# Q, K and V of two blocks by seven block products, in a phase of their own

## The chip, the cores and the metric

The kernel runs on one core of a Trainium2 chip. Its time is the device time of one execution in microseconds (us). Five engines work side by side, each through its own instructions in order: TensorE (PE, matmuls; its weight loads are shown as PEld), VectorE (DVE), ScalarE (ACT), GpSimd (POOL) and SyncE (SP, which here only issues DMAs). They wait for each other by semaphores.

## The reference

One transformer block whose attention and feed-forward parts are both added to the input (S = 2048 tokens, D = 576, 32 heads of 18, F = 4608, float32):

```python
xn = layernorm(x)
q, k, v = split_heads(xn @ wqkv)              # wqkv: 576 x 1728
# each token attends to itself and 7 earlier ones, 2 apart (0, 2, ..., 14 back)
attn = softmax(q . k[pos - 2 w] * 18 ** -0.5)  # masked where pos - 2 w < 0
a = (sum over w of attn * v[pos - 2 w]) @ wo
h = relu(xn @ w1 + b1) ** 2                    # 4608 wide
out = x + a + h @ w2 + b2
```

## The kernel before

**Numbers in two parts.** Matmuls read float32 in a rounded form (F32R). To keep the precision, an operand v is split into hi = rounded v (a ScalarE copy) and lo = v - hi (a DVE subtraction), and a product is hi*hi + lo*hi + hi*lo: three matmuls. So every weight that TensorE reads costs one ScalarE and one DVE operation: `w2_hi`/`w2_lo` for a tile of w2, `h_hi`/`h_lo` for a pair of tiles of the hidden activations that comes back from DRAM, `wq_hi`/`wq_lo` for wqkv.

**Tiles.** The 2048 tokens are four blocks of 512 (b = 0 to 3). D = 576 is four chunks of 128 and a left part of 64 (`x4`), which carries hi and lo in its 128 rows. wqkv is in four groups g of eight heads, 432 columns each (q, k and v of 144). The result is kept transposed, so that out is D x S.

**FFN1** (`ffn_pair`, L524 and L528) takes two blocks at a time and multiplies [two blocks] x [two halves of D] x [two tiles of w1] as a 2 x 2 by 2 x 2 block product in seven products instead of eight. It needs sums of blocks of x (`sums`, `last_sum`: SS[1..3], the fourth in X[b1][:, :, :2]) and of the weights (`combine_w1`; the slots T1, T3, B11, T2, B22, B21, T4), and some additions on the way out. FFN2 (`tile_products`, L493) is plain: 14 matmuls of 512 columns for each of the 36 tiles of F.

**The order.** It is written out by hand. Each engine does its instructions in the order of the code:

1. `open_rows` and `q0`: Q, K, V of blocks 0 and 1 (`qkv_row`, L304).
2. `phase_a(0)`: FFN1 of blocks 0 and 1 in 18 pairs of tiles, with FFN2 of block 0 in between; the activations of block 1 go to DRAM (`hscr`). Then Wo of block 0 and `finish(0)`: five drains on DVE (L747) of the sums in PSUM into the residual, and the stores.
3. `phase_b0`: FFN2 of block 1 over 36 tiles n, from DRAM, and in between the 32 rows of Q, K, V of blocks 2 and 3 (2 blocks x 4 groups x 4 row tiles j; 14 matmuls of 432 columns each, then a ScalarE copy into `st` and a DMA to `kvq`, L296 and L298). Then Wo of block 1; its last products and `finish(1)` are handed to the next phase as a `filler`.
4. `phase_a(1)`: the same as 2 for blocks 2 and 3.
5. `phase_b1`: FFN2 of block 3, Wo, and the end.

**What fills DVE.** Attention reads q, k and v of one block and group from DRAM (`kvq`) and works on DVE alone but for the exponential. `attention(b, g)` is a generator of 18 steps: four of q-k product (L95, `pr<-q,kv`) and four reductions (L353), two of softmax, four weightings (`pr<-lg,kv`) and four sums with the output. `side(k)` takes the next k steps from a queue of such generators; `complete(b)` forces all that is left of a block; then `regroup(b, .)` loads the output back and `o_hi`/`o_lo` turn it for Wo. `run(pieces, k)` takes k steps from a list `pieces` of other generators first: in `phase_b0` these are `normalize(2)`, the load of the statistics `mb` of block 3, `normalize(3)` (8 steps each), the splits of wqkv, and `sums(1)` (12 steps). Every tile n there takes `w2_hi`, `h_hi` (even n), the 14 matmuls, `w2_lo`, `h_lo` (even n), and then the steps of `run`. The buffers `w2s`, `h` and `w1s` are three deep, `w1r` two, `r4` four; PSUM has eight banks (`bank(0..7)`), and FFN2's sums of block 1 hold 5, 6, 7, 0, 1 (`YB`).

In `phase_b0` the rows are let in by the line

```python
while r < 32 and 32 * (n - 6) > 22 * r:
```

so from tile 7 to tile 28, more than one a tile.

Of the kernel before, what the change touches and what calls it, by code (L numbers as in the profile page):

```python
# [8 lines left out]
F32 = mybir.dt.float32  # L9
# [3 lines left out]
ALU = mybir.AluOpType  # L13
# [32 lines left out]
def block_kernel(ctx: ExitStack, tc: tile.TileContext, x, xt, wqkv, wo, w1, b1, w2, b2, out):  # L46
# [47 lines left out]
    def tt(out, a, b, op):  # L94
        return nc.vector.tensor_tensor(out=out, in0=a, in1=b, op=op)  # L95
# [196 lines left out]
    def open_stage():  # L292
        stage[0] = sb.tile([P, NJ, QW], F32, name="st")
# [93 lines left out]
    def side(k, exp=True):  # L387

        while k > 0:
            if current[0] is None:  # L390
                if not queue or queue[0][0] not in landed:
                    return k
                name, make = queue.pop(0)
                current[:] = [make(), None, name]
            if current[1] == "exp" and not exp:
                return k
            try:
                current[1] = next(current[0])
                k -= 1
            except StopIteration:  # L400
                current[0] = None
        return 0
# [17 lines left out]
    def once(f, *a):  # L420
        f(*a)
        return
        yield
# [80 lines left out]
    def ffn_pair(s, p, work, first=False):  # L504
# [179 lines left out]
    ob = {}  # L684

    def regroup(b, k):
        if k == 0:
# [6 lines left out]
    ot, of = {}, {}  # L694

    def o_hi(b, c):
        if c % 2 == 0:
            ot[b, c // 2] = mt.tile([P, 2, 2, TB], F32R, name="w1s", bufs=3)
# [8 lines left out]
        nc.vector.transpose(t[:, 0].rearrange("p (u k f) -> p u k f", k=2, f=n),  # L707
                            ob[b, 1][:, :, None, OB - n:].to_broadcast([P, NJ * G, 2, n]))
        nc.scalar.activation(t[:, 1].bitcast(F32R), t[:, 0], AF.Copy)

    def o_lo(b, c):
        hi, lo = (ot[b, c // 2][:, c % 2, k] for k in range(2))
        t = of.pop((b, c))
        if c < NC - 1:
            tt(lo, t[:, 0], hi.bitcast(F32), ALU.subtract)
# [19 lines left out]
    def open_left(b):  # L735
        xr[b].append(four()[:, 0])
# [7 lines left out]
    def drain(b, c, ts=slice(0, TB)):  # L744
        n = P if c < NC - 1 else D - DM
        o = kept(b, c, ts)
        i = nc.vector.scalar_tensor_tensor(out=o, in0=yp[b][c][:n, ts], scalar=b2t[:n, c:c + 1], in1=o,  # L747
                                           op0=ALU.add, op1=ALU.add)
        if c == NC - 1:
            i = tt(o, yp[b][c][n:2 * n, ts], o, ALU.add)  # L750
        return i

    def finish(b):
        for c in range(NC):
            drain(b, c)
# [13 lines left out]
    def h_lo(s, p):  # L769
        if p < NP:  # L770
            t = hs[s, p]
            tt(t[:, 1], t[:, 1].bitcast(F32), t[:, 0].bitcast(F32), ALU.subtract)

    def phase_b0():
        b, r = 1, 0
        todo = [(2 + i, g, j) for g in range(G) for i in range(2) for j in range(NJ)]
        split_up.clear()
        open_stage()
        load_wq(0)
        pieces = [normalize(2), once(load_mb, 3), split_wq(0, "S", lambda: load_wq(1)), normalize(3)]  # L780
        open_y(b)
        for n in range(NF):
            w2_hi()
            if n % 2 == 0:
                h_hi(0, n // 2 + 1)
            add(b, tile_products(b, n, hs[0, n // 2]))
            w2_lo()
            if n % 2 == 0:
                h_lo(0, n // 2 + 1)
            if n % 2 and n // 2 + 3 < NP:  # L790
                load_h(0, n // 2 + 3)
            run(pieces, 1 + n % 2 if n < 9 else 1)
            while r < 32 and 32 * (n - 6) > 22 * r:
                bb, g, j = todo[r]
                while bb not in normed or g not in split_up:
                    run(pieces, 1)
                qkv_row(bb, g, j, 2 + r % 3)
                r += 1
                if r == 2:
                    pieces.append(split_wq(1, "w1s", lambda: load_wq(2)))  # L800
                if r == 8:
                    pieces.append(split_wq(2, "S", lambda: load_wq(3)))
                if r == 16:
                    pieces.append(split_wq(3, "w1s"))
                if r == 24:
                    pieces.append(sums(1))
                if j == NJ - 1 and bb == 2:
                    offer(2, g)
                run(pieces, 2)
            if n == 3:  # L810
                load_xt(3)
            if n == 20:
                load_w1(NP)
            if n == 25:
                assert not any(a != "x" and c < 2 for a, c, _ in loads)
                held[0] = True
            if n == 28:
                run_all(pieces)
                last_sum(1)
                complete(1)  # L820
                regroup(b, 0)
                regroup(b, 1)
                held[0] = False
                fetch()
                load_w1(NP + 1)
                for g in range(G):
                    offer(3, g)
            if n == 31:
                combine_w1(NP)
            if n == 33:  # L830
                residual(b)
            if n in (32, 33):
                c = 2 * (n - 32)
                o_hi(b, c), o_hi(b, c + 1)
                o_lo(b, c), o_lo(b, c + 1)
        o_hi(b, 4)
        o_lo(b, 4)
        open_left(b)
        load_left(b)
        for c in range(3):  # L840
            w2_hi()
            add(b, o_ops(b, c))
            w2_lo()
            if c == 1:
                w1_hi(NP, 0)
                w1_lo(NP, 0)

        def filler(i):
            if i < 2:
                add(b, o_ops(b, 3 + i), range(NC) if i else ())  # L850
            if i == 0:
                w1_hi(NP, 1)
                w1_lo(NP, 1)
            if i == 1:
                finish(b)

        return filler

# [379 lines left out]
```

## Time and profile before

| | us |
|---|---|
| median of 3 runs | 1127.12 (1125.72 to 1128.43) |
| profiled execution | 1125.13 |
| its span | 1123.4 |
| PE / PEld / DVE / ACT busy | 1112.8 / 938.1 / 914.7 / 575.7 |
| FFN2 of block 1 with the QKV rows | about 436.6 to 640.7 |

In the profile, "L95" is the helper `tt` (any DVE operation of two tensors), "L493" the matmuls of FFN2 and Wo, "L304" those of `qkv_row`. A row of a group has: line, engine, operation, tile written <- tiles read, shapes, count | busy us, mean ns of one | idle time of the engine just before them and what ended it. A row of a wait has: who <- for whom, total us, times, longest. A row of a window has: its start and end, length, then busy time of PE, PEld, DVE, ACT and POOL with instruction counts, the granted clock of TensorE (1.00 is full), the share of the DMA engines and GB/s. A row of the timeline has: start, duration, engine, line, and in brackets the idle time before it and what ended it. A row of the chain has start, duration and what; in the view of a tile one row gives the time of its DMAs from issue to landing.

### The profile page before, as it was taken

The page shows a single profiled execution, that of the slowest core. Times are in us where ns is not written, and L with a number is a line of the kernel's source. Part 1 is how long each engine was busy: PE and PEld are TensorE (multiplying, and loading weights), DVE is VectorE, ACT ScalarE, POOL GpSimd, SP SyncE. Part 2 cuts the span into 40 slices and gives each one's busy share as a digit, 9 for nine tenths or more (in the row PEclk, how much of TensorE's full clock was granted, in tenths as well). Part 3 has the DMA queues.
Part 4 walks back from the last instruction along what each step waited for, and adds up shares of the span by engine and source line. Part 5 has one row for each costly group of instructions (what it writes and reads, how often), then busy time and mean ns, then how long its engine had stood idle before and what let it go on. Part 6 is the DMA issues. An engine that isn't in the chain of part 4 may idle for free.

```text
span 1123.4 us, 13847 instructions
## 1 busy us (share of the span) xinstructions
PE 1112.8 (99%) x5014; PEld 938.1 (84%) x5014; DVE 914.7 (81%) x1202; ACT 575.7 (51%) x801; POOL 117.7 (10%) x219
## 2 busy tenths in 40 slices
PE   8999999999999999999999999999999999999998
PEld 7998888888888888899888888888888888888887
DVE  6696998897978887789888979898988988786463
ACT  5434656656566654542342455666556666533341
POOL 4000201020300210002011001020202011001000
PEclk9999999999999999999999999999999999999999
DMA  8854645384573648766674845354545362568653
GB/s 292 310 188 130 203 162 199 111 212 155 175 198 104 252 180 303 257 231 213 215 247 145 318 154 194 144 172 149 202 140 203 112 217 94 186 200 305 181 169 90
DMA packets 88965, 216.50 MB, mean 193 GB/s; under 512 B 11960, under 2 KB 40384, under 8 KB 83520
## 3 DMA queue, kind: packets, MB, share of 16 engines
q1 hardware_dynamic: 52464, 148.95, 39.0%
q0 software_dynamic: 10544, 52.14, 14.4%
q10 hardware_dynamic: 25888, 14.53, 4.3%
q8 instruction: 39, 0.64, 0.2%
q14 instruction: 30, 0.25, 0.1%
HBM read 173.03 MB, written 42.55 MB: 192 GB/s over the span
## 4 chain that ended last, share of the span: by engine, by line
PE 87%; DVE 6%; DMA 3%; ACT 2%; issue 1%; SPq 0%; ACTq 0%; POOL 0%; DVEq 0%; POOLq 0%
PE p L493 42%; PE p L524 29%; PE p L304 9%; PE p L528 5%; DVE pr L95 1%; PE p L1022 1%; DMA kvq<-st 1%; DVE w1s L95 1%; DMA kv<-kvq 1%; DMA w2r<-in_w 1%; DVE r L95 1%; DVE lg L353 0%; DVE w1r L95 0%; DVE w2s L95 0%; DMA r<-in_wqkv 0%
## 5 line engine op out<-in xcount | busy, mean ns | idle before, releaser
L493 PE MATMUL p<-h,w2s 128*128 128x512 f32 x2010 | 484.4, 390 | 0.7 <-ACT h L535 0.2
L493 PEld LDWEIGHTS p<-h,w2s 128*128 128x128 f32 x2010 | 376.8, 188 | 81.2 <-ACT h L535 1.2
L524 PE MATMUL p<-X,w1s 128*128 128x512 f32 x864 | 219.5, 389 | 2.6 <-DVE w1s L95 2.6
L524 PEld LDWEIGHTS p<-X,w1s 128*128 128x128 f32 x864 | 162.1, 188 | 36.5 <-DVE w1s L95 3.0
L466 ACT ACTIVATE w2s<-w2r 128x640 fp32r<-128x640 f32 x164 | 120.1, 734 | 110.6 <-PE p L493 92.9
L95 DVE TENSOR_TENSOR w2s<-w2r,w2s 128x576 fp32r<-128x576 f32 x164 | 123.4, 754 | 63.8 <-ACT w2s L466 61.7
L524 PE MATMUL p<-S,w1s 128*128 128x512 f32 x648 | 164.6, 389 | 0.0
L524 PEld LDWEIGHTS p<-S,w1s 128*128 128x128 f32 x648 | 121.4, 188 | 25.5 <-DVE r L95 0.2
L381 POOL DMA_DIRECT2D o<-q x128 | 69.3, 606 | 606.5 <-DVE q L95 604.6
L95 DVE TENSOR_TENSOR w1s<-w1r,w1s 128x1024 fp32r<-128x1024 f32 x72 | 88.0, 1223 | 27.7 <-ACT w1s L439 27.6
L531 ACT ACTIVATE r<-r,b1t 128x512 f32<-128x512 f32 x72 | 51.9, 721 | 105.8 <-DVE r L95 105.7
L95 DVE TENSOR_TENSOR pr<-q,kv 128x1152 f32<-128x1152 f32 x64 | 86.8, 1356 | 1.5
L296 ACT ACTIVATE st<-p 128x432 f32<-128x432 f32 x64 | 33.8, 528 | 104.5 <-PE p L304 89.7
L95 DVE TENSOR_TENSOR pr<-lg,kv 128x1152 f32<-128x1152 f32 x64 | 86.6, 1353 | 0.7
L353 DVE TENSOR_REDUCE lg<-pr 128x64 f32<-128x1152 f32 x64 | 86.4, 1349 | 0.9
L95 DVE TENSOR_TENSOR pr<-pr 128x576 f32<-128x576 f32 (+1 forms) x128 | 77.7, 607 | 3.8
L439 ACT ACTIVATE w1s<-w1r 128x1024 fp32r<-128x1024 f32 x72 | 75.7, 1052 | 5.1 <-PE p L493 4.2
L539 ACT ACTIVATE r<-r 128x1024 f32<-128x1024 f32 x72 | 75.5, 1051 | 0.1
L95 DVE TENSOR_TENSOR h<-r,h 128x1024 fp32r<-128x1024 f32 (+2 forms) x42 | 49.2, 1180 | 30.2 <-ACT r L539 23.7
L528 PE MATMUL p<-x,w1s 128*128 128x512 f32 x216 | 66.5, 389 | 0.0
L95 DVE TENSOR_TENSOR r<-p,r 128x512 f32<-128x512 f32 (+1 forms) x76 | 52.2, 687 | 13.2 <-ACT r L589 10.3
L304 PE MATMUL p<-w1s,X 128*128 128x432 f32 x288 | 60.3, 358 | 0.0
(138 smaller groups left out, 1114.0 us busy)
## 6 DMA issues: line engine op xcount, KB each, us to landing
w2r<-in_w SPq DMA_DIRECT2D x144, 320.0 KB, 3.2
kv<-kvq POOLq DMA_DIRECT2D x29, 1296.0 KB, 6.8
w1r<-in_w SPq DMA_DIRECT2D x36, 640.0 KB, 4.4
h<-r SPq DMA_DIRECT2D x36, 512.0 KB, 2.9
h<-h SPq DMA_DIRECT2D x36, 512.0 KB, 4.1
kvq<-st ACTq DMA_DIRECT2D x64, 216.0 KB, 3.1
r<-in_wqkv SPq DMA_DIRECT2D x16, 432.0 KB, 5.5
w2r<-in_wo SPq DMA_DIRECT2D x20, 320.0 KB, 3.0
```

What stands on the lines that cost most here:

```text
L95: return nc.vector.tensor_tensor(out=out, in0=a, in1=b, op=op)
L296: nc.scalar.activation(stage[0][:, j], p[:, :QW], AF.Copy)
L304: nc.tensor.matmul(p[:, :QW], l, r, start=k == 0, stop=k == len(mm) - 1)
L353: nc.vector.tensor_reduce(out=lg[:, j * HG:(j + 1) * HG].rearrange("p a w -> p w a"), in_=pr.rearrange("p w (a d) -> p w a d", d=DH), axis ...
L381: nc.gpsimd.dma_start(rows[:, i], q[i * L:(i + 1) * L, :, a:z])
L439: nc.scalar.activation(w1s[n, k][:, 0], raw1[n][:, 4 * k:4 * k + 4], AF.Copy)
L466: nc.scalar.activation(w2s[stream[i]][:, :DE], raw2[i], AF.Copy)
L493: nc.tensor.matmul(yp[b][c], v, a, start=c not in yb[b], stop=c in last and c not in [o[0] for o in ops[i + 1:]], skip_group_check=True)
L524: nc.tensor.matmul(to, l, r, start=start and i == 0, stop=i == len(mm) - 1, skip_group_check=True)
L528: nc.tensor.matmul(to, weight(LEFT, k, f), v, start=False, stop=k == 1, skip_group_check=True)
L531: nc.scalar.activation(to, a, AF.Relu, bias=b1t[:, f:f + 1])
L539: nc.scalar.activation(r, r, AF.Square)
```

## The change

The 32 rows leave the loop of FFN2 of block 1. Behind that loop comes a phase of its own for Q, K, V of blocks 2 and 3: [block 2, block 3] x [two halves of D] x [groups 2k, 2k + 1] by the same seven products that FFN1 uses, for k = 0, 1 and each of the four row tiles j. `quad_step(k, s, j, i)` does step s for one j; two j run side by side (i = 0, 1), in banks 2, 3, 4, 0 and 5, 6, 7, 1. So a "half" is two row tiles of one k, and there are four halves. The sums of x are those that FFN1 needs anyhow; the weights are combined and split into eight slots on DVE and ScalarE (`first_slots`, `third_slot`, `split_slot`, `split_side`), for k = 0 within the FFN2 loop, for k = 1 during the phase.

As the phase takes all eight banks, the sums of FFN2 of block 1 are drained first into the residual, go to DRAM (`yscr`, `yleft`), and come back before Wo of block 1, which then adds without the bias (`finish(b, False)`). Attention of block 1 gives up to one more step a pair in FFN1 of blocks 0 and 1 (`side(3)`), and its `complete(1)` comes in the second half of the phase; block 2 is offered from there on, block 3 behind the phase. The splits of w1 for the next FFN1 move into the phase. `regroup(1)` uses one `kv` buffer, and `o_hi` of block 1 `h` buffers.

The diff, cut to its core:

```diff
         if not first:
-            side(1 if p == 1 else 2 + p % 2, False)
+            side(1 if p == 1 else 2 + p % 2 if s else 3, False)
...
+    def first_slots(k):
+        v, b12 = raw[k, 0][:, 0], raw[k, 0][:, 1]
+        b21, b22 = raw[k, 1][:, 0], raw[k, 1][:, 1]
+        if not k:
+            split_slot(B11, v)
+            yield
+        tt(v, b12, v, ALU.subtract)
+        yield
+        split_slot(T1, v)
+        yield
+        tt(v, b22, v, ALU.subtract)
+        yield
+        split_slot(T2, v)
+        yield
+        tt(v, b21, v, ALU.subtract)
+        yield
+
+    def third_slot(k):
+        v = raw[k, 0][:, 1]
+        tt(v, raw[k, 1][:, 1], v, ALU.subtract)
+        split_slot(T3, v)
...
+    def quad_step(k, s, j, i):
...
+        def product(to, name, v, start=False):
+            mm = [(v(0, n), ws[name][0][:, n]) for n in range(2)]
+            for n in range(2):
+                mm += [(v(0, n), ws[name][1][:, n]), (v(1, n), ws[name][0][:, n])]
...
+        def row(n, f, x, y=None):
+            st = stage[0][:, rows_out[0] % NJ]
+            rows_out[0] += 1
+            nc.scalar.activation(st, x, AF.Copy)
+            if y is not None:
+                tt(st, y, st, ALU.add)
...
+        if s == 1:
+            product(a, B11, lambda h, q: X[b0][:, h, q], start=True)
+            nc.scalar.activation(b, a, AF.Copy)
+        if s == 2:
+            product(c, T1, ss(1), start=True)
+        if s == 3:
+            product(b, T2, ss(2))
+            nc.scalar.activation(u, b, AF.Copy)
+        if s == 4:
+            left(c, 1, x4[b1])
+            product(b, T3, ss(3))
+            row(b1, 1, b, c)
+        if s == 5:
+            product(a, B21, lambda h, q: X[b0][:, h, 2 + q])
+            left(a, 0, x4[b0])
+            row(b0, 0, a)
+        if s == 6:
+            product(c, B22, lambda h, q: X[b1][:, h, q])
+            left(c, 1, x4["d"])
+            row(b0, 1, c, u)
+        if s == 7:
+            product(b, T4, lambda h, q: X[b1][:, h, 2 + q])
+            left(b, 0, x4[b1])
+            row(b1, 0, b)
...
     def phase_b0():
...
-        pieces = [normalize(2), once(load_mb, 3), split_wq(0, "S", lambda: load_wq(1)), normalize(3)]
+        pieces = [normalize(2), once(load_half, 0, 0), once(load_mb, 3), normalize(3), once(load_sides, 0), sums(1),
+                  once(load_half, 0, 1), once(last_sum, 1), first_slots(0), once(third_slot, 0),
+                  once(split_side, 0, 0), once(split_side, 0, 1)]
...
-            run(pieces, 1 + n % 2 if n < 9 else 1)
-            while r < 32 and 32 * (n - 6) > 22 * r:
...
+            run(pieces, 1 + n % 2)
...
             if n == 33:
                 residual(b)
+                xr[b].append(sb.tile([P, TB], F32, name="xf"))
+                load_left(b)
+            if n == 34:
+                split_slot(B21, raw[0, 1][:, 0])
+        for c in range(NC):
+            drain(b, c)
+            if c in (1, 3):
+                nc.sync.dma_start(yscr[:, c - 1:c + 1], xr[b][0][:, c - 1:c + 1])
+        nc.sync.dma_start(yleft, kept(b, NC - 1))
+        open_stage()
...
+        for k in range(2):
+            for half in range(2):
+                for s, i in ((1, 0), (1, 1), (2, 0), (2, 1), (3, 0), (3, 1), (5, 0), (4, 0), (5, 1), (4, 1),
+                             (7, 0), (6, 0), (7, 1), (6, 1)):
+                    quad_step(k, s, 2 * half + i, i)
+                    hook(k, half, s, i)
+                    if (s, i) in ((2, 0), (2, 1), (3, 0), (5, 0), (5, 1), (4, 1), (7, 0), (7, 1)) and (k, half) != (0, 1):
+                        side(1, s == 7)
...
+        xr[b] = [mt.tile([P, NC - 1, TB], F32, name="h", bufs=3)]
+        nc.sync.dma_start(xr[b][0], yscr)
+        open_y(b)
         for c in range(3):
             w2_hi()
             add(b, o_ops(b, c))
             w2_lo()
...
             if i == 1:
-                finish(b)
+                finish(b, False)
```

`hook` puts the loads and splits of the weights of k = 1, T4 and B22 of k = 0, `complete(1)`, the offers of block 2, and the first work for Wo of block 1 and for the next FFN1 behind single steps of the phase: in the first half T4 behind step 1 and B22 behind step 5 (i = 0), in the second half the slots of k = 1.

More of the change, by code (lines that the diff above doesn't have):

```diff
@@ L686, in regroup @@
     def regroup(b, k):
+        if b == 1:
+            assert free[0]
+            free[0] -= 1
+            t = sb.tile([P, NJ * G * CG], F32, name="kv", bufs=3)
+            for i, n in enumerate((OA, OB)):
+                ob[b, i] = t[:, i * NJ * G * OA:][:, :NJ * G * n].rearrange("p (r c) -> p r c", c=n)
+                nc.gpsimd.dma_start(t[:, i * NJ * G * OA:][:, :NJ * G * n], oscr[b, i].rearrange("p r c -> p (r c)"))
+            return
         if k == 0:
@@ L772, in h_lo, with load_half, load_sides @@
             tt(t[:, 1], t[:, 1].bitcast(F32), t[:, 0].bitcast(F32), ALU.subtract)
+    raw, ws, yscr = {}, {}, dram.tile([P, NC - 1, TB], F32, name="y1")
+    yleft = dram.tile([D - DM, TB], F32, name="y1e")
+    def load_half(k, i):
+        t = raw[k, i] = sb.tile([P, 2, 2, QW], F32, name="w1r", bufs=2)
+        for f in range(2):
+            nc.sync.dma_start(t[:, f], wqkv[2 * k + f, :, 2 * i:2 * i + 2])
+    def load_sides(k):
+        t = raw[k, "left"] = sb.tile([P, 2, QW], F32, name="mb")
+        for f in range(2):
+            nc.sync.dma_start(t[:, f], wqkv[2 * k + f, :, NC - 1])
@@ new lines, in slot, with split_slot, split_side @@
+    def slot(name):
+        if name == B11:
+            ws[name] = [four(F32R)[:, :, :QW] for _ in range(2)]
+        else:
+            t = mt.tile([P, 2, 2, TB], F32R, name="w1s" if name in (T1, T2, T3) else "h", bufs=3)
+            ws[name] = [t[:, i, :, :QW] for i in range(2)]
+        return ws[name]
+    def split_slot(name, v):
+        split(*slot(name), v)
+    def split_side(k, f):
+        t = ws[LEFT, f] = four(F32R)[:, :, :QW]
+        split(t[:, 0], t[:, 1], raw[k, "left"][:, f])
@@ new lines, in phase_b0 @@
+        for k in range(2):
[6 more added lines that the diff above has]
+                        side(1, s == 7)
+                    if (s, i) in ((2, 1), (5, 0), (7, 0)) and (k, half) == (0, 1):
+                        side(1, s == 7)
@@ L840, in phase_b0 @@
+        for g in (2, 3):
+            offer(2, g)
+        for g in range(G):
+            offer(3, g)
+        xr[b] = [mt.tile([P, NC - 1, TB], F32, name="h", bufs=3)]
+        nc.sync.dma_start(xr[b][0], yscr)
+        open_y(b)
         for c in range(3):
```

147 lines of the change are left out of this document (87 added, 60 removed).

## The prediction

> **What bounds the kernel now.** I read the page first, then the chain of waits in order of time, the waits of each engine, and the groups of instructions by form for VectorE (DVE).
>
> ```profile
> PE 1112.8 (99%) x5014; PEld 938.1 (84%) x5014; DVE 914.7 (81%) x1202; ACT 575.7 (51%) x801; POOL 117.7 (10%) x219
> PE p L524 <- DVE w1s L95: 2.6, 1, 2.6
> ...
> 615.69 2.75 PE p L304 x14
> 618.44 22.25 PE p L493 x98
> ```
>
> TensorE is busy for 99% of the span, and its longest wait for data in the middle of the kernel is 2.6 us. So time comes off only with matmuls. One QKV row (14 matmuls of 432 columns, L304) takes 2.75 us, 196 ns each; a tile of FFN2 (14 matmuls of 512, L493) takes 22.25 / 7 = 3.18 us. The other half of the reading is DVE in the stage that changes:
>
> ```profile
> 440.00:640.60 200.60, 200.45 (x941) 176.39 (x939) 174.90 (x202) 78.83 (x114) 19.55 (x36) 1.00 0.69 236
> ```
>
> In FFN2 of block 1 with QKV of blocks 2 and 3 strewn in, TensorE (second number) never waits, but DVE (fourth) is busy for 174.9 of 200.6 us: 87%, with 26 us to spare. TensorE is slow enough for DVE only because of the QKV rows.
>
> **The matmuls removed.** Before: 2 blocks x 4 groups x 4 row tiles x 14 = 448 matmuls. After: 8 calls of the seven products x (7 x 6 + 8 for the left part) = 400. Forty-eight fewer at 196 ns: **-9.4 us**, all of it on TensorE's path.
>
> **What DVE has to do before the new phase can start.** The banks 5, 6, 7, 0, 1 of FFN2's sums are needed by the new phase; its second product (step 1 with i = 1) writes bank 5, which only DVE's first drain frees. DVE works in order, so that drain stands behind everything queued in the 36 tiles. TensorE's own road to that product is 36 x 3.18 + 6 x 0.196 = 115.7 us from the first FFN2 matmul (436.6 us). DVE's road I add up. Its start is the same list as before, up to the end of `normalize(2)`, and the trace shows it:
>
> ```profile
> 436.55 2.72 DVE L747 SCALAR_TENSOR_TENSOR w1r<-p,b2t,w1r 128x512 f32<-128x512 f32 x4
> ...
> 449.24 1.22 DVE L95 TENSOR_TENSOR w1r<-w1r,mb 128x1024 f32<-128x1024 f32 x1
> 452.21 0.76 DVE L95 TENSOR_TENSOR w2s<-w2r,w2s 128x576 fp32r<-128x576 f32 x1 [1.75 <-ACT w2s L466]
> ...
> 459.63 0.69 DVE L95 TENSOR_TENSOR x<-xf,x 64x512 fp32r<-64x512 f32 x1
> 460.35 1.06 DVE L95 TENSOR_TENSOR S<-r,S 128x864 fp32r<-128x864 f32 x1
> DVE w2s L95 <- ACT w2s L466: 2.6, 3, 1.8
> DVE h L95 <- ACT h L767: 0.4, 2, 0.2
> ```
>
> That is 23.8 us for six tiles' worth: block 0's drains, six `w2_lo`, three `h_lo`, one `normalize`, and 3.0 us of waits for ScalarE. Their durations add to 21.7, so 0.9 overlaps (4%). What follows, by form:
>
> ```profile
> L95 DVE TENSOR_TENSOR w2s<-w2r,w2s 128x576 fp32r<-128x576 f32 x164 | 123.4, 754 | 63.8 <-ACT w2s L466 61.7 <-PE p L304 1.3 <-issue 0.2
> L95 DVE TENSOR_TENSOR h<-h 128x1024 fp32r<-128x1024 f32 x36 | 44.0, 1223 | 5.4 <-ACT h L767 5.1 <-DMA kvq<-st 0.2
> L95 DVE TENSOR_TENSOR w1r<-w1r,mb 128x1024 f32<-128x1024 f32 x12 | 14.4, 1220 | 2.3 <-DMA mb<-mr 2.1
> L95 DVE TENSOR_TENSOR r<-r,mb 128x512 f32<-128x512 f32 x2 | 1.4, 688 | 0.0
> L95 DVE TENSOR_TENSOR S<-r,S 128x864 fp32r<-128x864 f32 x6 | 6.2, 1055 | 5.1 <-ACT S L262 5.1
> L95 DVE TENSOR_TENSOR S<-r,S 128x432 fp32r<-128x432 f32 x3 | 1.8, 604 | 0.5 <-ACT S L262 0.5
> L95 DVE TENSOR_TENSOR pr<-q,kv 128x1152 f32<-128x1152 f32 x64 | 86.8, 1356 | 1.5
> L353 DVE TENSOR_REDUCE lg<-pr 128x64 f32<-128x1152 f32 x64 | 86.4, 1349 | 0.9
> L95 DVE TENSOR_TENSOR pr<-lg,kv 128x1152 f32<-128x1152 f32 x64 | 86.6, 1353 | 0.7
> L95 DVE TENSOR_TENSOR pr<-pr 128x576 f32<-128x576 f32 (+1 forms) x128 | 77.7, 607 | 3.8
> L95 DVE TENSOR_TENSOR q<-pr 128x144 f32<-128x144 f32 x64 | 19.7, 308 | 2.2
> L363 DVE TENSOR_REDUCE sm<-lg 128x32 f32<-128x256 f32 x16 | 6.7, 418 | 6.6 <-ACT lg L361 6.6
> L95 DVE TENSOR_TENSOR lg<-lg,mx 128x256 f32<-128x256 f32 x16 | 6.8, 425 | 0.5
> 414.29 1.36 DVE L95 TENSOR_TENSOR pr<-q,kv 128x1152 f32<-128x1152 f32 x1
> ```
>
> - 30 `w2_lo` x 0.754 = 22.6; 14 `h_lo` x 1.223 = 17.1.
> - `normalize(3)`: six operations of 1024 at 1.22 and three of 512 at 0.69 = 9.4.
> - `sums(1)`, `last_sum`: eleven of 1024 and two of 512 = 14.8.
> - The weight slots B11, T1, T2, T3, B21: five differences `lo` and four weight differences of 864 at 1.055, and two sides of 432 at 0.604 = 10.7.
> - Attention. The loop takes 1 + n % 2 steps a tile, 54 in all; the list uses 34 (8 + 8 + 12 + 6) and leaves 20. Before, when FFN1 of blocks 0 and 1 ends, attention of block 1 stands at the first step of its third group (the q-k product at 414.29), and counting the yields of the generators gives the same place; with `side(3)` in the even pairs the place is 7 steps further on. The 20 steps are then two softmaxes, four q-k with reductions, four weightings with sums: 4 x (1.356 + 1.349 + 1.353 + 2 x 0.607 + 0.308) + 2 x 2.04 (five operations of about 0.41) = 26.4.
>
> Together 101.0, less 4% overlap 97.0. To this come two waits that the list makes:
>
> *The statistics of block 3.* `normalize(3)` follows `normalize(2)` at once, and its first operation needs `mb`, whose load stands on SP behind two new loads of 432 KB.
>
> ```profile
> 460.05 0.38 SPq L762 DMA_DIRECT2D h<-h  x1
> 460.48 0.42 SPq L172 DMA_DIRECT2D mb<-mr  x1
> DVE w1r L95 <- DMA mb<-mr: 1.8, 1, 1.8
> DMA to landing us min/median/max: 6.7/6.8/8.7
> 436.00:463.00 27.00, 23.93 (x28) 1.00 0.81 280
> ```
>
> Before, DVE filled that time with the first weight split and still waited 1.8 us. After, SP reaches `mb` two issues later, about 461.3; 6.7 us more is 468.0, a wait of 7.7 us from 460.3; 864 KB ahead of it at the window's 280 GB/s make 3.1 more, 10.8. I take 10. The Trainium skill ("DMA: Bandwidth & Descriptors", Anatomy of one DMA) puts a transfer at about 2.0 us plus its bytes over 436 GB/s. By it the three would need an estimated 5.2 us, the wait would be about 6 and the sum 4 us less; the trace's 6.7 for `mb` alone, against 3.2 by that fit, disagrees.
>
> *ScalarE in between.* ScalarE is in order too. Where a tile's last step ends with a copy on ScalarE, the next `w2_hi` stands behind the copy, and DVE waits for both: the 1.75 us at 452.21. This happens when DVE is what lags. `normalize(3)` meets it three times (5 us), `sums` three times (5); the splits of T2 and T3 follow their own difference at once (1 each), the two softmaxes cost 0.55 each (6.6 us for 12 waits), `h_hi` about 1: 14, between 5 (most of it met by time already lost) and 18.
>
> DVE's road: 23.8 + 97.0 + 10 + 14 = 144.8, and the first drain 0.7: 145.5 against TensorE's 115.7. TensorE cannot keep ahead, since `w2s` and `h` are three deep: the hi part for tile n + 2 is freed by tile n - 1, so it can lead DVE by about two tiles, 6.4 us. Behind the last `w2_lo` that TensorE needs, DVE has about 9 us of steps before the first drain, and TensorE only 3.2 us of work (2 of FFN2, 1.2 of the first product): some 5.5 us of the loss show as a wait at the new phase's start, the rest as waits inside FFN2. **+29.8 us**; with the ends of the two waits, 12.8 + 5 below and 10.8 + 18 above, +18 to +35.
>
> **The new phase itself.** Each half has 100 matmuls, 19.6 us. DVE there: half 1 the five drains (4.2), T4 and B22 (2.1), eight steps (11.5), four additions (about 2.5) = 20.3; half 2 the slots of k = 1, 15.5; halves 3 and 4 some 14 each. Its additions free a bank only 24 matmuls (4.7 us) later, so a lag of that size is hidden: nothing in the middle, up to 3 us if half 1 runs late. Sums to DRAM: two stores of 512 KB, under way 5.8 us after the drains begin, before the slot that they hold is wanted by B22 (about 7.5). The load back has the 13 us of Wo. At the end, bank 7 and bank 1 wait for a ScalarE copy (528 ns) and an addition: **+0.6**. Attention of blocks 2 and 3 moves behind: FFN1 is as full as before (DVE 88%), and FFN2 of block 3 gets steps for 20 tiles instead of 10. There two tiles cost DVE about 6.8 us against 6.36: **+0.5**, between 0 and 2, hidden by the same lead. `side(3)` in FFN1 of block 0: nothing, DVE has 14% spare there.
>
> ```profile
> L296 ACT ACTIVATE st<-p 128x432 f32<-128x432 f32 x64 | 33.8, 528 | 104.5 <-PE p L304 89.7 <-DMA kvq<-st 10.8 <-ACT st L296 2.4
> 200.00:300.00 100.00, 100.00 (x443) 82.81 (x442) 86.08 (x139) 60.67 (x81) 16.21 (x27) 1.00 0.52 154
> 880.00:940.00 60.00, 60.00 (x266) 49.71 (x265) 52.98 (x70) 36.23 (x49) 5.97 (x11) 1.00 0.43 144
> ```
>
> **The sum.** -9.4 + 29.8 + 0.6 + 0.5 = +21.5 us. The profiled execution took 1125.13 us; the median of the runs is 1127.12, 2 us above it. So 1146.6 on the profile's time, **1148.6 us** as a median.
>
> **The rivals.**
>
> *The waits are met by other time.* If `mb` lands without a wait and ScalarE is always ahead, DVE's road is 23.8 - 3.0 + 97.0 + 0.7 = 118.5, and the loss 2.8 us: -9.4 + 2.8 + 1.1 = -5.5, 1121.6, faster. It decides where all waits of DVE in that road come to less than about 5.5 us. For it: a stretch behind the QKV rows where DVE works 95% of the time and TensorE does not wait. Against: `mb` never landed in under 6.7 us. Chance 0.09, of which 0.03 within 0.2%.
>
> ```profile
> 618.30:640.70 22.40, 22.40 (x99) 18.19 (x97) 21.31 (x28) 10.63 (x16) 2.71 (x5) 1.00 0.85 328
> ```
>
> *The waits are at their lower ends* (7.7 and 5): 134.2 us of road, loss 18.5, +10.2, 1137. Chance 0.17.
>
> *The clock falls in the gaps.* The kernel's first matmuls, after 2.1 us of idleness, took 2.74 / 6 = 457 ns for 512 columns, twice the 227 of FFN2's, for about 4.5 us.
>
> ```profile
> 2.14 2.74 PE L939 MATMUL p<-lg 128*128 128x512 bf16 x6 [2.14 <-DVE lg L932]
> 97.00:100.00 3.00, 2.52 (x11) 1.00 0.17 23
> ```
>
> If the wait for `mb` (about 7 us on TensorE) and the one at the phase's start (5.5) each bring that back, each costs 2.3 us more: 1153. The granted clock stayed at 1.00 behind the gap of 2.6 us near 97, which is shorter. The Trainium skill ("TensorE: Matmul & The Clock Gate", Why this matters for your kernels) warns of idle gaps over about 3 us, after which the clock halves; no run here shows such a gap in mid-kernel. Chance 0.13.
>
> *The seven products save nothing*, as 432-column matmuls could be paced by the 188 ns weight load of each: then the count still falls by 48. I see no way for it; 0.01.
>
> **How the numbers follow.** The forecast has 0.56, with its own range 1138 to 1156. Beyond it, a late first half and the high ends make 1157 to 1165: 0.04. Eight in ten: 1131 to 1158; that leaves out the first rival and the high tail, and holds cases where part of ScalarE's waits vanish too. A measurement here tells about 0.2% (2.3 us) from no change. Faster 0.06, same 0.03, slower 0.91.
>
> **What would show it.** Right: TensorE's busy time in all down by about 9 us while its waits for DVE in the FFN2 lines of block 1 grow to over 20 us; DVE near 90% there with one wait of about 10 us for `mb`; a wait of some 5.5 us for the first drain ahead of the new phase; that phase about 78 us long. Wrong: FFN2 of block 1 in under 120 us, `mb` awaited for under 4 us, or the new phase itself far over 82.

## The result and the profile after

The changed kernel takes 1146.62 us (median of 4 runs, 1146.22 to 1147.24) against 1126.62 us for the kernel before on the same chip (4 runs, 1125.72 to 1128.43): ratio 1.0176, interval 1.0158 to 1.0194. It is slower, by 20.0 us. The profiled execution took 1146.9 us, its span 1145.2 against 1123.4.

First the page of the changed kernel: the busy times and the granted clock in 40 slices.

```profile
PE 1113.7 (97%) x4966; PEld 932.8 (81%) x4966; DVE 936.2 (82%) x1238; ACT 586.9 (51%) x823; POOL 116.9 (10%) x219
PEclk9999999999999999899989999999999999999999
```

There are 48 matmuls fewer, as counted, but TensorE's share fell from 99 to 97% and its busy time didn't fall at all. The clock row has two digits under 9 in the middle; before it had none.

The windows below cut the changed stage in three: FFN2 of block 1 (with the last three matmuls of Wo of block 0), the turn from it to the new phase, and the phase from its second product to Wo. The columns are as in the window rows of before.

```profile
438.78:576.70 137.92, 122.24 (x507) 97.17 (x506) 111.15 (x129) 56.06 (x72) 4.35 (x8) 0.96 0.56 184
576.70:583.05 6.35, 1.43 (x8) 0.99 (x7) 5.73 (x11) 0.84 (x2) 0.00 (x0) 0.81 0.69 225
583.05:662.52 79.47, 79.47 (x394) 75.82 (x395) 55.59 (x72) 35.11 (x62) 8.10 (x15) 0.97 0.70 223
```

FFN2's first matmul starts at 439.13 us. From there to Wo it takes 662.52 - 439.13 = 223.4 us; before it took 640.72 - 436.62 = 204.1. That is +19.3 of the +21.8 in span. Behind Wo both kernels need 482.7 us. The other 2.5 us lie ahead of 439.13: TensorE's wait in FFN1 near 96 us was 3.06 instead of 2.57 us, with a stretch of half clock behind it, and there were two waits of 1.4 us in all near 253 and 271. In later runs with the same code up to there, FFN2 of block 1 began at 436.0 us (experiment 10) and at 439.7 (experiment 12), so I do not put these 2.5 us down to the change.

What TensorE waited for in the changed stage (waits after; total, times, longest):

```profile
PE p L493 <- ACT h L779: 7.8, 6, 3.1
PE p L493 <- DVE w2s L95: 5.8, 1, 5.8
PE p L851 <- DVE h L759: 4.9, 1, 4.9
PE p L493 <- ACT w2s L466: 2.0, 3, 1.0
```

L493 is FFN2, L851 the new phase, L759 the drains. Two of the rows name ScalarE, but ScalarE was 59% idle there: its copies stood behind others that wait for DVE. What DVE waited for between the first drain of block 0 and the first of block 1 says where that began:

```profile
DVE w2s L95 <- ACT w2s L466: 15.1, 11, 2.4
DVE w1r L95 <- DMA mb<-mr: 7.7, 1, 7.7
DVE w1r L95 <- DMA w1r<-in_wqkv: 2.0, 1, 2.0
DVE w1s L95 <- ACT w1s L99: 2.0, 2, 1.0
DVE sm L363 <- ACT lg L361: 1.0, 2, 0.5
DVE h L95 <- ACT h L779: 0.9, 5, 0.2
```

The two drains and the `mb` wait in DVE's timeline, then the start of the phase's second product on TensorE (in brackets the idle time before it):

```profile
438.74 2.72 DVE L759 SCALAR_TENSOR_TENSOR w1r<-p,b2t,w1r 128x512 f32<-128x512 f32 x4
470.23 1.23 DVE L95 TENSOR_TENSOR w1r<-w1r,mb 128x1024 f32<-128x1024 f32 x1 [7.71 <-DMA mb<-mr]
582.25 2.73 DVE L759 SCALAR_TENSOR_TENSOR h<-p,b2t,h 128x512 f32<-128x512 f32 x4
```

```profile
583.05 2.53 PE L851 MATMUL p<-r,X 128*128 128x432 f32 x6 [4.92 <-DVE h L759]
663.31 9.64 PE L493 MATMUL p<-h,w2s 128*128 128x512 f32 x40 [0.16 <-ACT st L860]
```

DVE's road is 582.25 - 438.74 = 143.5 us, and TensorE starts the product that it frees 583.05 - 439.13 = 143.9 us after FFN2's first matmul. Its own road is 115.7.

### The profile page after: what moved, and what is told of

Its sections match the earlier page's. It is cut to its first block, busy times and chain, and to the rows that moved or that the text cites. A ratio compares the mean times of both kernels' runs of the same rounds, so it can differ in the third digit from the quotient of the medians.

```text
span 1145.2 us, 13847 instructions
## 1 busy us (share of the span) xinstructions
PE 1113.7 (97%) x4966; PEld 932.8 (81%) x4966; DVE 936.2 (82%) x1238; ACT 586.9 (51%) x823; POOL 116.9 (10%) x219
## 4 chain that ended last, share of the span: by engine, by line
PE 76%; DVE 13%; DMA 4%; issue 3%; ACT 3%; POOL 0%; SPq 0%; ACTq 0%; DVEq 0%; POOLq 0%
PE p L493 35%; PE p L524 26%; PE p L851 6%; PE p L528 5%; DVE pr L95 3%; DVE w1r L95 2%; DMA w2r<-in_w 2%; PE p L304 1%; DVE h L95 1%; DVE w2s L95 1%; PE p L855 1%; DVE w1s L95 1%; PE p L1180 1%; DVE lg L353 1%; DMA kvq<-st 1%
## 5 line engine op out<-in xcount | busy, mean ns | idle before, releaser
L493 PE MATMUL p<-h,w2s 128*128 128x512 f32 x2066 | 500.7, 393 | 16.0 <-ACT h L779 7.8
L493 PEld LDWEIGHTS p<-h,w2s 128*128 128x128 f32 x2066 | 389.6, 189 | 104.4 <-ACT h L779 10.3
L95 DVE TENSOR_TENSOR w1s<-w1r,w1s 128x1024 fp32r<-128x1024 f32 (+1 forms) x78 | 94.2, 1209 | 27.0 <-ACT w1s L439 20.1
L95 DVE TENSOR_TENSOR h<-r,h 128x1024 fp32r<-128x1024 f32 (+3 forms) x46 | 51.8, 1137 | 30.8 <-ACT r L539 23.4
L95 DVE TENSOR_TENSOR w1r<-w1r 128x256 f32<-128x256 f32 (+3 forms) x118 | 66.1, 560 | 4.6 <-DMA w1r<-in_wqkv 2.0
L568 ACT ACTIVATE r<-p 128x512 f32<-128x512 f32 x36 | 21.6, 600 | 68.7 <-PE p L524 68.7
```

What stands on the lines that cost most here:

```text
L493: nc.tensor.matmul(yp[b][c], v, a, start=c not in yb[b], stop=c in last and c not in [o[0] for o in ops[i + 1:]], skip_group_check=True)
L568: nc.scalar.activation(u[:, 0], bb, AF.Copy)
```

## The experiments

The theory: the gain is the 9.4 us of matmuls; DVE's road sets the start of the new phase, and its queued work and waits cost some 29 us. Rivals: the loss is in the phase itself; or it is TensorE's clock; or the attention steps that were pushed forward in FFN1 cost something. All edits are against the changed kernel or the one named, and the ratios are to the kernel before on the same chip.

**1. The load of `mb` early.** It goes to the start of the FFN2 loop, into the buffer `st`, which is free there.

```diff
-        mb[b] = sb.tile([P, 2, TB], F32, name="mb")
+        mb[b] = sb.tile([P, 2, TB], F32, name="st" if b == 3 else "mb")
...
-        pieces = [normalize(2), once(load_half, 0, 0), once(load_mb, 3), normalize(3), ...
+        pieces = [normalize(2), once(load_half, 0, 0), normalize(3), ...
...
+        load_mb(3)
         for n in range(NF):
```

> The statistics of block 3 are loaded at the start of FFN2 of block 1 into the tile 'st', which is idle there, instead of behind the two weight loads. Theory (DVE's queue of work sets when the new phase can start, 143.5 us from the first drain of block 0 to the first drain of block 1): the 7.7 us wait for mb goes and everything behind it comes 7.7 us sooner: 1146.6 - 7.7 = 1139, between 1137.5 and 1140. Rival (ScalarE's chain is the bound, it has the largest sum of TensorE's waits, 7.8 + 2.0 us): only TensorE's one wait of 5.8 us for DVE goes and is partly made up: 1141 to 1146. Rival (the halved clock behind long gaps): one of three half-clock stretches goes, about 2 us: 1144.5.

Measured: 1136.87 us, ratio 1.0103 (1.0077 to 1.0129), 9.8 us less than the changed kernel. In the profile of this run the way from FFN2's first matmul to Wo takes 216.2 us, 7.2 less than the 223.4 of the changed kernel: that is what the wait of 7.7 us is worth. The rest of the difference is not this edit's: FFN2 began at 435.9 us instead of 439.1, behind the same code.

**2. ScalarE ahead.** The hi parts of the next tile are issued before the steps of `run`.

```diff
+        w2_hi()
+        h_hi(0, 1)
         for n in range(NF):
-            w2_hi()
-            if n % 2 == 0:
-                h_hi(0, n // 2 + 1)
...
+            if n < NF - 1:
+                w2_hi()
+                if n % 2:
+                    h_hi(0, n // 2 + 2)
             run(pieces, 1 + n % 2)
```

> In FFN2 of block 1 the splits w2_hi and h_hi of the next tile are put ahead of the tile's steps, so that they do not stand behind a copy on ScalarE that waits for DVE. Same work. Theory: of the 15.1 us that DVE waits for w2s on ScalarE in this stage some 13 go, and the time falls by as much: 1133.5, between 1131 and 1137. Rival (DVE's waits for ScalarE are met by other waits): under 5 us of gain, 1142 or more.

Measured: 1133.17 us, 1.0063 (1.0042 to 1.0085), 13.5 us less. The order in which ScalarE gets its copies, with not one operation more or less, costs more than the change gains.

**3. Both.**

> Both edits. Theory: DVE's road from drain to drain falls to 143.5 - 7.7 - 13 = 122.8 us, still longer than TensorE's 115.7, so the gains add: 1146.6 - 20.7 = 1126, between 1123 and 1129, about the kernel before. Rival (hand-over of the sums through DRAM and the phase change cost the time): 1139 or more, since neither edit touches them.

Measured: 1127.39 us, 1.0011 (0.9999 to 1.0022), 19.2 us less than the changed kernel. Alone the two gave 9.8 + 13.5 = 23.2. From FFN2's first matmul to Wo the profiles of the three runs are shorter by 7.2, 12.2 and 18.1 us, so there the two nearly add up and share 1.3. TensorE's waits in FFN2 and ahead of the phase:

```profile
PE p L851 <- DVE h L759: 4.1, 1, 4.1
PE p L493 <- DVE w2s L95: 3.3, 1, 3.3
```

DVE's road was 125.9 us. Of the 9.4 us, these waits take 7.4, and slower matmuls more than the rest: TensorE's busy time is 1108.0 us here, 3.7 above that of experiment 10, which ran at full clock.

```profile
PE 1108.0 (98%) x4966; PEld 931.9 (83%) x4966; DVE 935.3 (83%) x1238; ACT 588.4 (52%) x823; POOL 116.5 (10%) x219
```

**4. Without the extra attention steps in FFN1.**

```diff
-            side(1 if p == 1 else 2 + p % 2 if s else 3, False)
+            side(1 if p == 1 else 2 + p % 2, False)
```

> side(3) in the even pairs of FFN1 of blocks 0 and 1 goes back to side(2); seven steps of block 1's attention then fall into the second half of the new phase. Theory: TensorE's two waits of 1.4 us for DVE's additions in FFN1 near 253 and 271 us go, and DVE has room in the second half: 1146.6 - 1.4 = 1145.2, between 1144 and 1146. Rival (the seven steps, about 10 us of DVE, make the second half of the new phase late): 1148 to 1152.

Measured: 1168.82 us, 1.0382 (1.0359 to 1.0405): 22.2 us more, against the theory's small gain and beyond the rival. The timelines of GpSimd, DVE and TensorE show why:

```profile
636.86 4.31 POOL L381 DMA_DIRECT2D o<-q  x8 [57.67 <-DVE q L95]
644.29 0.54 POOL L326 DMA_DIRECT2D kv<-kvq  x1
651.56 1.36 DVE L95 TENSOR_TENSOR pr<-q,kv 128x1152 f32<-128x1152 f32 x1 [15.00 <-DMA kv<-kvq]
657.66 2.53 PE L851 MATMUL p<-h,X 128*128 128x432 f32 x6 [19.03 <-DVE st L95]
```

Seven steps late, the last output of block 1 is stored at 637 us. The load of block 2's k rows stands on GpSimd's queue behind that store and behind `regroup(1)`. DVE meets the first step of block 2 before the rows are there and stops for 15 us; the phase's own additions into `st` are queued behind it, and TensorE waits for those for 19 us.

**5. and 6. Work moved to GpSimd.** Both edits of 3, with eleven splits and differences of the weights of k = 0 on GpSimd, between single steps of the loop, and 20 (then 28) attention steps in it.

```diff
+        def less(o, a, c):
+            nc.gpsimd.tensor_tensor(out=o, in0=a, in1=c, op=ALU.subtract)
+        def split_pool(hi, lo, v):
+            nc.scalar.activation(hi, v, AF.Copy)
+            less(lo, v, hi.bitcast(F32))
...
-                  once(load_half, 0, 1), once(last_sum, 1), first_slots(0), once(third_slot, 0),
-                  once(split_side, 0, 0), once(split_side, 0, 1)]
+                  once(load_half, 0, 1), once(last_sum, 1), pool_slots()]
```

> On top of the two edits of e3_both, the lo parts and differences of the first weight slots (B11, T1, T2, T3, the sides, B21) go from DVE to GpSimd, spread over twice as many tiles; the steps of attention in the FFN2 loop stay 20. The same arithmetic. GpSimd took 1.125 us for 432 columns, DVE 0.6: about 22 us on GpSimd, which is idle there. Theory: DVE's road from drain to drain falls from 125.9 us by 10.7 x 0.96 + 2.0 (waits for T2, T3) + 2 to about 112 to 114, under TensorE's 115.7; what is left of the loss is the drain itself, 1 to 2 us: 1126 - 9.4 + 1.5 + 0.5 = 1118.5, between 1116.5 and 1121.5; faster than the kernel before. Rival (the hand-over through DRAM and the banks costs what is left): no gain over e3_both, 1127. Rival (ScalarE stuck behind GpSimd's slow differences): 1128 or more.

> e5_pool with 28 instead of 20 steps of attention in the FFN2 loop; the eight come out of the first half of the new phase. Theory: DVE's road grows by 8 x 1.38 = 11 us to about 124 and is the bound again: e5_pool + 8 to 11 us, near 1128. Rival (total work of DVE over loop and phase counts, not its place): the same as e5_pool within 2 us.

Measured: 1132.62 us, 1.0066 (1.0048 to 1.0083), and 1143.30, 1.0159 (1.0142 to 1.0177). The fifth missed by 14 us: with less work DVE was later. Rows of DVE and of GpSimd in the fifth, from the same stretch:

```profile
514.13 2.55 DVE L95 TENSOR_TENSOR w2s<-w2r,w2s 128x576 fp32r<-128x576 f32 x1
519.60 2.05 DVE L95 TENSOR_TENSOR q<-pr 128x144 f32<-128x144 f32 x1
513.06 3.00 POOL L905 TENSOR_TENSOR w1r<-w1r 128x864 f32<-128x864 f32 x1
519.33 4.18 POOL L905 TENSOR_TENSOR w1r<-w1r 128x864 f32<-128x864 f32 x2
PE p L493 <- DVE w2s L95: 10.8, 3, 5.7
```

The same two DVE operations take 0.75 and 0.31 us elsewhere. Each is longer by 1.7 to 1.8 us, a good part of one GpSimd operation, and the first ends just behind the one beside it (516.7 and 516.1 us): the two engines hold each other up. TensorE's wait for `w2s` grew from 3.3 to 10.8 us, though its wait for the first drain fell from 4.1 to 1.3. The time is in the range of the second rival (1128 or more), but not for its reason: DVE's waits for ScalarE on its road were 10.1 us against 10.8 in 3, while its busy time there rose from 115.0 to 119.2 us with fewer operations. The sixth came out as expected, 10.7 us above the fifth: DVE's road was 145.2 us instead of 132.7, so the eight steps moved into the loop cost their full DVE time there.

**7. As 4, with no attention steps in the third half,** so that nothing of the phase is behind the late k rows.

```diff
-... and (k, half) != (0, 1):
+... and (k, half) not in ((0, 1), (1, 0)):
```

> As e4_side_back, but without the eight steps of block 2's attention in the third half of the new phase. In e4 the first of them waited 15.0 us for its k rows on DVE, with the additions of the new phase queued behind it, and TensorE waited 19.0 us for those. Theory: the k rows land before the fourth half begins; the 19 us go, with the half clock behind them (20 us at half in the clock records, about 1 to 3 us of it in matmuls): 1168.8 - 20 to 22 = 1148, between 1146 and 1151. Rival (the seven late steps themselves block the phase): 1160 or more.

Measured: 1160.92 us, 1.0318 (1.0296 to 1.034). That is 7.9 us under the fourth, but far from 1148. DVE still met the rows before they came, in the fourth half:

```profile
DVE pr L95 <- DMA kv<-kvq: 9.3, 1, 9.3
```

The time is the one that the rival gave (1160 or more), but as DVE still waits for rows, this run does not tell the two causes apart; 9 and 10 do. The phase took 86.3 us, and the part from Wo on 491.9 instead of 482.7. Most of these 9 us are lost at once: in the first 29.2 us of Wo TensorE did 101 matmuls, the changed kernel 128 in 29.5, as it waited 2.9 us for the phase's late additions and copies and the granted clock was 0.88.

**8. The order in tile 19.** As 3, but in the tile where the list does `last_sum`, the steps are issued before the hi parts again: in 3 DVE waited 4.3 us there for a copy that stood behind one that waits for TensorE.

```profile
DVE X L95 <- ACT X L99: 4.3, 1, 4.3
```

```diff
+            if n == 19:
+                run(pieces, 1 + n % 2)
             if n < NF - 1:
                 w2_hi()
...
-            run(pieces, 1 + n % 2)
+            if n != 19:
+                run(pieces, 1 + n % 2)
```

> Both edits of the third experiment, and in tile 19 the list's steps stand ahead of the next tile's hi parts again, so that ScalarE's copy for `last_sum` isn't behind a copy that waits for TensorE. Theory (DVE's road sets the start of the new phase): the wait of 4.3 us for `X` shrinks to about 1, DVE's road falls from 125.9 to about 122.7 us, and the time from 1127.4 to about 1124. Rival (TensorE was the one that was late there, and DVE only waited for it): no change, 1127.

Measured: 1125.35 us, 0.9993 (0.9982 to 1.0003). DVE's road was 123.8 us, 2.1 less than in 3 where 3.2 were expected, and the time fell by 2.0.

**9. and 10. Three attention steps fewer in the loop.** As 8, with 17 steps; the three others stand in the second half of the phase, in 9 at the places that the kernel has for them, in 10 at its first three.

```diff
+        left_over = [17]
...
+            k = min(k, left_over[0])
+            left_over[0] -= k
+            side(k)
...
-                    if (s, i) in ((2, 1), (5, 0), (7, 0)) and (k, half) == (0, 1):
+                    if (s, i) in ((1, 0), (1, 1), (2, 0)) and (k, half) == (0, 1):
```

(The last two lines are the tenth's.)

> As the one before, and only 17 of the 20 attention steps in the FFN2 loop of block 1; the other three go into the second half of the new phase, whose three places for such steps find nothing to do now. Theory: DVE's road falls by another 3.9 us (a reduction 1.35, a softmax 2.0 with its wait of 0.5) to about 118.8 us against TensorE's 116.4; TensorE's waits in FFN2 and ahead of the phase come to 2 to 3 us in all instead of 7.4, and the time to about 1121 us, 0.4% under the kernel before: what is left of the 9.4 us that the 48 matmuls save. Rival (the steps in the new phase make the sums late, as in the fourth experiment): TensorE waits for `st` by several us and the time stays at 1124 or more.

> As the ninth experiment, but the three attention steps stand behind steps (1,0), (1,1) and (2,0) of the second half of the new phase instead of (2,1), (5,0) and (7,0), so that block 1's last outputs go to GpSimd's queue some 15 us earlier, as early as in the eighth. Theory (the ninth was slow only because the k rows of block 2 were queued behind those outputs): the wait of 15.2 us for `kv` and TensorE's 12.3 us for `st` are gone, TensorE waits about 4 us in FFN2 of block 1 and ahead of the phase, and the time is 1122 to 1124 us, under the kernel before by 0.2 to 0.4%. Rival (the number of steps in the phase is what delays it, wherever they stand): 1130 or more.

Measured: 1138.57 us, 1.011 (1.0096 to 1.0124), and 1124.96, 0.9993 (0.9982 to 1.0004). In the ninth the waits in FFN2 and for the drain fell to 4.1 us, where 2 to 3 were expected, and the fault of the fourth came back, as the rival has it (waits of DVE and TensorE):

```profile
DVE pr L95 <- DMA kv<-kvq: 15.2, 1, 15.2
PE p L851 <- DVE st L95: 12.3, 2, 11.7
PE p L851 <- DVE h L759: 3.3, 1, 3.3
```

In the tenth, with the same work some 15 us earlier, DVE's wait for `kv` is 0.6 us and TensorE's for DVE's `st` is gone. That is what the theory says of the fourth and the ninth: what counts is when block 1's last output enters GpSimd's queue. The time is a little above the 1122 to 1124 expected, and cannot be told from that of the kernel before; the granted clock was 0.995 to 0.998 in ten of its runs, and 1.00 in two, which took 1120.9 and 1121.6 us. The profiled run is one of these two, so its matmuls can be compared with those of before:

```profile
PE 1104.3 (99%) x4966; PEld 926.7 (83%) x4966; DVE 935.4 (84%) x1238; ACT 588.5 (53%) x823; POOL 116.5 (10%) x219
PE p L851 <- DVE h L759: 3.5, 1, 3.5
```

TensorE is busy for 8.5 us less than before.

**11. and 12. Other products first.** As 10, but the first half begins with steps (1,0), (2,0), (3,0), whose products go to banks that FFN2 did not hold. In 12 the first three attention steps of that half also stand behind (1,1), (2,1), (3,1).

```diff
-                for s, i in ((1, 0), (1, 1), (2, 0), (2, 1), (3, 0), (3, 1), (5, 0),
+                first = (((1, 0), (2, 0), (3, 0), (1, 1), (2, 1), (3, 1)) if (k, half) == (0, 0) else
+                         ((1, 0), (1, 1), (2, 0), (2, 1), (3, 0), (3, 1)))
+                for s, i in (*first, (5, 0),
...
+                    early = ((1, 1), (2, 1), (3, 1)) if (k, half) == (0, 0) else ((2, 0), (2, 1), (3, 0))
```

> As the tenth experiment, and the new phase starts with three products of the banks that FFN2 never held, (1,0), (2,0), (3,0), before the first one into bank 5, (1,1). Theory: 12 more matmuls, 2.4 us, stand ahead of the first drain, so that TensorE's wait for it falls from 3.5 to about 1.1 us; the stretch of half clock behind it (worth 1.2 us, in most runs of the tenth) goes as well. 1121 to 1122.5 us against 1125.0 for the tenth, 0.3 to 0.4% under the kernel before. Rival (the copy of step (3,0) into bank 0 waits on ScalarE for the fourth drain and holds up the copy that step (3,1) needs): a wait of 1 to 2 us moves there, and the time stays at 1123 to 1125.

> As the eleventh experiment, and the first three attention steps of the first half stand behind (1,1), (2,1) and (3,1) instead of (2,0), (2,1) and (3,0), so that the softmax's exponential is again behind the copy of step (1,1) on ScalarE. Theory (the eleventh lost its gain only to that exponential): the wait of 3.6 us for the copy falls to about 0.5, TensorE's waits between FFN2 of block 1 and the middle of the phase come to about 3 us in all, and the time to 1122 to 1123.5 us, 0.2 to 0.35% under the kernel before. Rival (the copy of (3,0) behind the fourth drain is what holds it up): a wait of 2 to 3 us stays at (3,1), and the time is 1124 to 1127.

Measured: 1127.48 us, 1.0013 (1.0002 to 1.0025), and 1123.23, 0.998 (0.9969 to 0.9991). In the eleventh the wait for the drain fell to 0.6 us, and a new one took its place, at step (3,1) (first row). ScalarE had the exponential of an attention step in its queue ahead of the copy that this step needs (second row, its timeline), and that exponential waits for DVE, which waits behind the drains.

```profile
PE p L851 <- ACT p L869: 3.9, 2, 3.6
564.57 0.42 ACT L361 ACTIVATE lg<-lg 128x256 f32<-128x256 f32 x1 [2.98 <-DVE lg L95]
```

The twelfth takes that away; TensorE's waits of this stage are then as follows (the last row is the first drain in DVE's timeline):

```profile
PE p L851 <- ACT st L860: 1.9, 2, 1.0
PE p L851 <- DVE h L759: 1.5, 1, 1.5
PE p L493 <- DVE w2s L95: 0.8, 1, 0.8
PE p L851 <- DVE st L95: 0.6, 1, 0.6
PE p L851 <- ACT p L869: 0.5, 2, 0.3
560.95 2.73 DVE L759 SCALAR_TENSOR_TENSOR h<-p,b2t,h 128x512 f32<-128x512 f32 x4 [2.03 <-DMA h<-in_xt]
```

It is the one version whose interval lies below 1, by 0.2% or 2 us: of the 9.4 us, some 5.3 are still lost to these waits, and some 2 to slower matmuls (TensorE's busy time in its profile is 1107.4 us, 3.1 above the tenth's). One interval of twelve, found by trying, is thin evidence; the profiles agree with it, as the way from FFN2's first matmul to Wo takes 201.4 us in the twelfth and 201.6 in the tenth against 204.1 before. The last row shows that DVE's queue no longer sets the first drain here: DVE stands idle for 2.0 us (1.6 in the tenth) until the load of the residual is there, which SyncE issued only 6.5 us before. An earlier issue of that load was not tried.

## Why the prediction was right

The forecast was +21.5 us and a median of 1148.6; measured were +21.8 in span (+20.0 in the medians) and 1146.6. That it came so close is in part luck: 2.5 of the 21.8 lie ahead of the changed stage, and there it is +19.3. It was right in its mechanism, and the sizes came out so:

- *The matmuls, -9.4.* Right to within 0.9 us. The changed profile hides it under slow matmuls; the tenth experiment, whose profile like that of before is at full clock, shows 8.5 us of busy time.
- *DVE's road, 144.8.* Measured 143.5, by errors that cancel. The wait for `mb` was 7.7 and not 10: its load was issued at 463.6 (first row below), which is 461.5 when the 2.2 us are taken off by which its first drain of block 0 is later than before, as worked out, and the data was there at 470.2, 6.6 us later. So the 864 KB ahead of it cost nothing, and the 3.1 us that I added for them were wrong. The Trainium skill ("DMA: Bandwidth & Descriptors", Anatomy of one DMA) states the fit that I set beside this for DMAs that GpSimd issues; this load is issued by SyncE, so it does not test the fit. The waits for ScalarE were 15.1 + 2.0 + 1.0 + 0.9 = 19.0, of which 3.0 were already in the first 23.8: 16.0 and not 14. A wait of 2.0 us for the second raw half of the weights was not in the sum. The work itself was 143.5 - 28.7 of waits = 114.8, against 23.8 - 3.0 + 97.0 = 117.8. The road cost 143.9 - 115.7 = +28.2 instead of +29.8. (The lower end of the two waits is written as 12.8 + 5 in the sum; it is 7.7 + 5, and that gives the +18.) Experiments 1 to 3 show that the two waits are its main part: taken away together, they give back 19.2 of it.
- *The first drain, 5.5 us of wait.* 4.9.
- *The phase, 78 us; hand-over to Wo +0.6; FFN2 of block 3 +0.5.* 79.5, of which 2.1 are slow matmuls at its start (below), 0.16 and nothing.
- *The waits in FFN2.* I gave over 20 us as the sign, with DVE near 90%; they were 15.6, and DVE 81% busy. The 90% was careless: a road of 145 us with 27 us of waits in it is 81%. The rest of TensorE's loss is slower matmuls, by the rival I gave 0.13:

```profile
463.62 0.43 SPq L172 DMA_DIRECT2D mb<-mr  x1
469.50:476.30 6.80, 4.12 (x10) 3.29 (x11) 4.32 (x5) 1.68 (x2) 0.00 (x0) 0.64 0.17 49
583.00:585.50 2.50, 2.45 (x7) 2.27 (x8) 2.50 (x4) 0.00 (x0) 0.00 (x0) 0.50 0.42 165
585.38 5.84 PE L851 MATMUL p<-w1s,S 128*128 128x432 f32 x24
558.95 4.86 PE L851 MATMUL p<-w1s,S 128*128 128x432 f32 x24
```

The clock did fall behind both gaps (the column after POOL: 0.64 and 0.50). I had priced that at 2.3 us each. Within FFN2 it cost nothing that shows (taking the wait for `mb` away in experiment 1 gave 7.2 us, not more than the wait itself), as DVE set the pace there and TensorE only waited less. At the phase's start, where TensorE sets it, the price was about right: six matmuls took 2.53 us, against 1.44 at the same place of the tenth experiment at full clock, and the next 24 took 5.84 against 4.86 (last two rows, the changed kernel and the tenth), 2.1 us together.

The step that failed is `side(3)`, priced at "nothing, DVE has 14% spare there". For the time of FFN1 that is near enough. But I costed the steps where they were put and not what they make room for: experiment 4 shows that without those seven steps the kernel is 22 us slower, as attention of block 1 then ends after the point where GpSimd's queue must turn to block 2. With that, the change's worst danger was in no line of the prediction, and the phase's "nothing in the middle" held only because of an edit that I had set at zero.

The rival on the other side (the waits are met by other time, 1121.6) needed a road without waits. Experiments 8, 10 and 12 come near it by hand, and the last reaches 1123.2.

## What to carry to other kernels

Where work leaves TensorE, add up the queue of the engine that frees its operands and its accumulators, waits included, and not only that engine's busy share; then look for the waits that an order of issue makes, since here one load issued earlier and ScalarE's copies issued ahead of the next steps gave back 19 of 28 us with no work removed. An in-order engine (DVE and ScalarE here, and GpSimd for its DMAs) passes a delay to everything queued behind it, so a step of side work must be placed by the latest time at which what it waits for is surely there.

## What the hardware showed that was not expected

GpSimd and DVE slow each other: DVE's subtraction of 576 columns took 2.55 us instead of 0.75, and its sum of 144 columns 2.05 instead of 0.31, while GpSimd ran subtractions of 864 columns, and these took 2.0 to 3.0 us each. The Trainium skill ("SBUF — State Buffer", Who interferes with whom) has it that a DVE instruction with two SBUF inputs contends with a GpSimd instruction that reads SBUF, and that the port pair that they share is held by an exclusive lock; the durations in experiment 5 agree with it.

The length of a gap alone does not decide the clock. Near 96 us every one of these kernels has the same wait of TensorE, behind the same code, of 2.4 to 3.4 us. Behind 3.06 us four matmuls of 512 took 2.07 us in the changed kernel; behind 2.46 they took 2.08 in experiment 4, at a granted clock of 0.50, but behind 3.35 only 1.20 in experiment 2, at 1.00. The first drain of the new phase shows the same: behind 3.46 us six matmuls took 1.44 us in experiment 10, behind 3.28 they took 2.53 in experiment 9. The Trainium skill ("TensorE: Matmul & The Clock Gate", Why this matters for your kernels) warns of gaps over about 3 us; here the clock could halve behind 2.46 us and could stay behind 3.46, so between these the length does not tell. Behind the gaps of 4.1 us and more ahead of a first drain (the changed kernel and experiments 1 to 4, 7 and 8) it was halved each time. The rows, of the changed kernel, experiments 4 and 2, 10 and 9:

```profile
96.56 2.07 PE L524 MATMUL p<-X,w1s 128*128 128x512 f32 x4 [3.06 <-DVE w1s L95]
96.43 2.08 PE L524 MATMUL p<-X,w1s 128*128 128x512 f32 x4 [2.46 <-DVE w1s L95]
97.86 1.20 PE L524 MATMUL p<-X,w1s 128*128 128x512 f32 x4 [3.35 <-DVE w1s L95]
557.68 1.44 PE L851 MATMUL p<-r,X 128*128 128x432 f32 x6 [3.46 <-DVE h L759]
560.26 2.53 PE L851 MATMUL p<-r,X 128*128 128x432 f32 x6 [3.28 <-DVE h L759]
```
